# Scratch buffers moved into the weight page, more of V kept between layers, and wo loaded in pieces between two layers

## The chip, the core and the metric

The kernel runs on one core of one Trainium2 chip. The metric is device time in microseconds (us), the median of several executions. The kernel before took 541.6 us (541.54 to 541.95 in five runs). TensorE is called PE here, VectorE DVE, ScalarE ACT, and SyncE, whose queue (SPq) issues the large loads, SP.

## The reference

The reference runs four steps on a single token of width 640, all in bf16: attention, a gated feed-forward block (FFN), and both again with the same weights.

```python
W = min(4096, max(256, Sk // 4))               # 4096 cached positions
k = k_cache[:, :, Sk - W:, :]                  # 32 heads x 4096 x 192
v = v_cache[:, :, Sk - W:, :]
q = (layernorm(x) @ wq), 32 heads of 192
x = x + softmax(q k^T / sqrt(192)) v @ wo
x = x + (silu(layernorm(x) @ w1) * (layernorm(x) @ w3)) @ w2
# ... and the same two lines once more
```

What matters: each layer reads 50.3 MB of K and 50.3 MB of V for one query per head, so nearly all the time goes into reading memory. K and V are the same for both layers. Whatever stays on the core from layer 0 need not be read again in layer 1.

## The kernel before

One large buffer `pg` (the page) holds all loaded data: a ring for weights and seven slots, each for one head pair's K or V (3.15 MB). Loads are queued in a fixed order by `plan`, and all are issued by SP. A load waits until the instructions that use the old contents of its place are done; every load behind it in the queue waits too.

```python
SLOT = 64 * DH
HALF = SLOT // 2
AUX = 10752
RING = AUX + HALF            # the ring runs over the first half of slot 0
NPG = AUX + NSLOT * SLOT
...
def need(key):               # issue the queued loads, in order, up to key
    while key not in place:
        k, at, n, src = queue.pop(0)
        ...
        nc.sync.dma_start(out=pg[:, at:at + n], in_=src)
```

Layer 0 handles head batches 0, 1, 2, 3 and layer 1 handles 3, 2, 1, 0, so the K and V of batch 3 can be kept. The K of batch 3 is kept whole (four slots), V of pairs 1 and 2 whole, V of pair 3 by half, V of pair 0 not at all. The ring overlaps the first half of slot 0, and that is why half of pair 3's V could not stay.

At the start of layer 1 the order of the queue and of PE is this:

```python
for half in (1, 0):                       # wq in ten pieces through the ring
    for c in range(NCH):
        ...plan(("wq", 1, half, c), ring(3072), 3072, ...)
plan_k(1, 2, 0, 1)                        # next K: into slot 1, where K of batch 3 pair 0 lies
plan_v(1, 3, 0, 3)
plan_k(1, 2, 1, 5)
plan_v(1, 3, 3, 0, CUT_V, kept=2)         # the half of V that was not kept
...
plan_cut(("wo", 1, 3), D, (12,), wo_v[3], 0)
...
layernorm()
q_mms(q_ps[1], 1, range(NCH))             # wq second half of the columns
qproj_tail(q_ps[1], 1)
q_mms(q_ps[0], 0, (0, 1))
build_w(order[0])
for z, cs in enumerate(((2, 3), (4,), (), ())):
    k_stage(order[0], z, s_ps, z == 0, z == NZ - 1)   # scores with the kept K, frees its slot
    q_mms(q_ps[0], 0, cs)
```

## Time and profile before

| | before |
|---|---|
| time, median | 541.6 us |
| span of the profiled run | 539.8 us |
| PE, DVE, ACT busy | 54%, 45%, 7% |
| read from HBM | 224.13 MB |
| chain of waits | 69% DMA |

Four lines of the profile's page of the kernel before. The first two belong to the view in 40 slices of 13.5 us: the busy share of the 16 DMA engines in tenths, and what they moved. Then come the bytes read, and the chain of waits by engine.

```profile
DMA  8999999999999999999999899999999999999995
GB/s 352 435 435 433 424 425 431 437 426 430 424 435 421 440 424 429 435 433 424 415 404 414 337 370 420 421 433 433 433 426 427 432 432 430 429 431 426 420 409 206
HBM read 224.13 MB, written 0.00 MB: 415 GB/s over the span
DMA 69%; DVE 13%; PE 12%; ACT 2%; issue 2%; SPq 1%; another core or an unknown queue 0%; ACTq 0%; DVEq 0%
```

The DMA engines are busy nearly all the time. The one place inside the run where they are not is slices 23 and 24 (337 and 370 GB/s, about 297 to 324 us), between the layers. The same stretch in windows of 2 us, of the kernel before; the columns are the window, its length, busy time and instruction counts of PE, PEld, DVE, ACT and POOL, the granted PE clock, the DMA share and GB/s.

```profile
272.00:274.00 2.00, 1.16 (x10) 0.47 (x10) 0.00 (x0) 0.48 (x1) 0.00 (x0) 0.50 0.99 400
274.00:276.00 2.00, 0.97 (x23) 0.83 (x22) 0.90 (x2) 0.00 (x0) 0.00 (x0) 0.50 1.02 420
...
306.00:308.00 2.00, 2.00 (x10) 0.67 (x8) 0.00 (x0) 0.00 (x0) 0.00 (x0) 0.50 0.78 323
308.00:310.00 2.00, 2.00 (x18) 0.80 (x16) 0.00 (x0) 0.00 (x0) 0.00 (x0) 0.85 0.19 73
310.00:312.00 2.00, 2.00 (x20) 0.96 (x16) 0.00 (x0) 0.00 (x0) 0.00 (x0) 1.00 0.51 135
312.00:314.00 2.00, 2.00 (x11) 0.64 (x9) 0.00 (x0) 0.00 (x0) 0.00 (x0) 1.00 0.69 283
314.00:316.00 2.00, 2.00 (x16) 0.76 (x14) 0.00 (x0) 0.00 (x0) 0.00 (x0) 1.00 0.93 393
```

The windows from 300 to 306 us, just before, show 415 to 424 GB/s. Against 420 GB/s the five windows from 306 to 316 us are short by (97 + 347 + 285 + 137 + 27) GB/s x 2 us = 1.79 MB. I call this shortfall "the gap" and work it out from the windows that fall short. A packet is counted whole in the window in which it begins, so a single window is coarse (one below reads 462 GB/s) and the sum over the stretch is what counts. The two windows at 272 us are shown because the change will touch them: here only 0.04 MB is missing there. When SP issued the loads around the gap, from the timeline of the kernel before (start, length, what, how many):

```profile
257.42 25.37 SPq L98 DMA_DIRECT2D pg<-in_B_w_dram  x9
285.30 16.40 SPq L98 DMA_DIRECT2D pg<-in_A_wq_dram  x10
310.46 0.56 SPq L98 DMA_DIRECT2D pg<-in_A_k_cache_dram  x1
```

Between the last wq load (issued by 301.7 us) and the next K load nothing is issued for 8.8 us. The K load needs slot 1, and PE frees it only when the scores of the first kept K block are done.

From 309.5 to 311.8 us no packet begins. The gap is therefore a queue that ran empty, not a slow transfer.

### The profile page before, as it was taken

To read this page: it belongs to the slowest core of one execution; us is meant where nothing else is said; L and a number is where in the kernel's file an instruction comes from. 1 tells how busy PE (TensorE), PEld (TensorE's weight loads), DVE (VectorE), ACT (ScalarE), POOL (GpSimd) and SP (SyncE) were. 2 spreads that over 40 slices of the span, in tenths; PEclk is the share of its full clock that TensorE was granted. 3 is DMA by queue.
4 is the path that set the end of the run, shared out by engine and by line. 5 is a ranking of instruction groups with operands and counts; after the bars stand their busy time and mean duration, and the time that the engine had idled before them with its cause. 6 is when DMAs were issued, how large, how long until landed. Compare 5 with 4: busy or idle time off the path is not lost.

```text
span 539.8 us, 6579 instructions
## 1 busy us (share of the span) xinstructions
PE 292.0 (54%) x2934; PEld 124.8 (23%) x2934; DVE 243.8 (45%) x274; ACT 37.8 (7%) x90; POOL 8.7 (2%) x38
## 2 busy tenths in 40 slices
PE   2427654450774335844456798762763415945365
PEld 1202111110321122213235232220321112312153
DVE  2179974417465265452011026776475075553010
ACT  1000020001100020002010002001100020002000
POOL 6000000000000000000000000000000000000000
PEclk9998797775777757976755599896688757868757
DMA  8999999999999999999999899999999999999995
GB/s 352 435 435 433 424 425 431 437 426 430 424 435 421 440 424 429 435 433 424 415 404 414 337 370 420 421 433 433 433 426 427 432 432 430 429 431 426 420 409 206
DMA packets 15294, 224.56 MB, mean 416 GB/s; under 512 B 1825, under 2 KB 1826, under 8 KB 6690
## 3 DMA queue, kind: packets, MB, share of 16 engines
q1 hardware_dynamic: 15122, 224.14, 97.9%
q8 instruction: 23, 0.38, 0.3%
q14 instruction: 5, 0.04, 0.0%
q10 hardware_dynamic: 144, 0.00, 0.0%
HBM read 224.13 MB, written 0.00 MB: 415 GB/s over the span
## 4 chain that ended last, share of the span: by engine, by line
DMA 69%; DVE 13%; PE 12%; ACT 2%; issue 2%; SPq 1%; another core or an unknown queue 0%; ACTq 0%; DVEq 0%
DMA pg<-in_A_k_cache_dram 51%; DMA pg<-in_A_wo_dram 12%; DVE pg L290 9%; PE s_ps L297 6%; DMA pg<-in_B_w_dram 4%; PE o_ps L340 2%; PE y_ps L372 2%; DMA pg<-in_A_wq_dram 2%; ACT e L315 1%; DVE et L319 1%; SPq L98 1%; DVE wst L282 1%; PE z_ps L437 1%; ACT ptm L328 1%; PE gu_ps L401 0%
## 5 line engine op out<-in xcount | busy, mean ns | idle before, releaser
L290 DVE STREAM_TRANSPOSE pg<-pg 128x1536 uint32<-128x1536 uint32 x112 | 189.2, 1746 | 122.5 <-DMA pg<-in_A_k_cache_dram 122.4
L297 PE MATMUL s_ps<-pg,wst 128*32 128x512 bf16 x768 | 175.5, 618 | 110.1 <-DVE pg L290 107.2
L297 PEld LDWEIGHTS <-wst 128*32 128x32 bf16 x768 | 48.4, 116 | 221.0 <-issue 205.1
L340 PE MATMUL o_ps<-pg,ptm 128*16 128x384 bf16 (+1 forms) x1024 | 73.2, 369 | 23.9 <-DMA pg<-in_A_v_cache_dram 21.0
L340 PEld LDWEIGHTS <-ptm 128*16 128x16 bf16 (+1 forms) x1024 | 30.4, 97 | 53.7 <-issue 39.2
L357 PE MATMUL ot_ps<-o_sb,csel 128*128 128x192 bf16 x16 | 3.5, 317 | 68.2 <-ACT o_sb L354 68.2
L315 ACT ACTIVATE e<-s_ps,nbt 32x512 bf16<-32x512 f32 x16 | 13.1, 821 | 376.6 <-DVE nbt L312 376.4
L372 PE MATMUL y_ps<-otd,pg 128*128 128x1 bf16 x540 | 23.1, 178 | 11.7 <-DVE otd L364 6.8
L372 PEld LDWEIGHTS <-pg 128*128 128x128 bf16 x540 | 23.1, 131 | 13.7 <-issue 9.3
L262 PE MATMUL q_ps<-pg,xs 128*32 128x384 bf16 x160 | 15.9, 491 | 11.6 <-DMA pg<-in_A_wq_dram 8.8
L361 DVE SCALAR_TENSOR_TENSOR om<-ot_ps,rl,dsel 128x192 f32<-128x192 f32 x8 | 3.1, 386 | 36.8 <-PE ot_ps L357 36.8
L349 DVE RECIPROCAL rl<-rl_ps 128x1 f32<-128x1 f32 x8 | 1.4, 169 | 38.7 <-PE rl_ps L347 38.7
L357 PEld LDWEIGHTS <-csel 128*128 128x128 bf16 x16 | 1.6, 100 | 71.8 <-issue 71.8
L319 DVE STREAM_TRANSPOSE et<-e 128x1024 bf16<-128x1024 bf16 x8 | 10.0, 1245 | 15.2 <-ACT e L315 15.2
L328 ACT COPY ptm<-et 32x256 bf16<-32x256 bf16 x32 | 13.6, 425 | 8.0 <-DVE et L319 7.5
L262 PEld LDWEIGHTS <-xs 128*32 128x32 bf16 x160 | 6.2, 123 | 18.7 <-issue 14.1
L303 DVE TENSOR_REDUCE t<-s_ps 128x1 f32<-128x512 f32 x8 | 5.2, 645 | 11.0 <-PE s_ps L297 11.0
L278 DVE CAST qt_sb<-qt_ps 128x96 bf16<-128x96 f32 x4 | 1.0, 257 | 19.6 <-PE qt_ps L275 19.6
L401 PE MATMUL gu_ps<-xs,pg 128*128 128x1 bf16 x120 | 8.1, 200 | 3.0 <-DMA pg<-in_B_w_dram 3.0
L330 DVE COPY ptm<-et 32x256 bf16<-32x256 bf16 x32 | 9.2, 287 | 0.6
L401 PEld LDWEIGHTS <-pg 128*128 128x128 bf16 x120 | 7.7, 166 | 4.1 <-DMA pg<-in_B_w_dram 4.1
L243 PE MATMUL st_ps<-xsq,onesD 128*128 128x12 f32 x8 | 2.4, 374 | 10.7 <-DVE xsq L241 10.7
(66 smaller groups left out, 77.4 us busy)
## 6 DMA issues: line engine op xcount, KB each, us to landing
pg<-in_A_k_cache_dram SPq DMA_DIRECT2D x28, 3072.0 KB, 41.1
pg<-in_A_v_cache_dram SPq DMA_DIRECT2D x27, 3072.0 KB, 37.0
pg<-in_A_wo_dram SPq DMA_DIRECT2D x6, 1920.0 KB, 34.5
pg<-in_A_wq_dram SPq DMA_DIRECT2D x10, 768.0 KB, 8.2
pg<-in_A_wq_dram SPq DMA_DIRECT2D x2, 3072.0 KB, 9.9
pg<-in_B_w_dram SPq DMA_DIRECT2D x8, 768.0 KB, 14.4
pg<-in_A_v_cache_dram SPq DMA_DIRECT2D x3, 1536.0 KB, 16.9
pg<-in_A_wo_dram SPq DMA_DIRECT2D x6, 640.0 KB, 24.1
```

Of the source, the lines that this page charges most:

```text
L98: nc.sync.dma_start(out=pg[:, at:at + n], in_=src)
L262: nc.tensor.matmul(q_ps[32 * j:32 * j + 32, 0:384], lhsT=xs4[:, c, c2, :], rhs=w[:, o:o + 384], start=(c == 0 and cl == 0), stop=(c == NCH ...
L282: nc.vector.tensor_tensor(out=_ap(wst[:], 0, P, 4 + 216 * h, [[433, NZ], [36, 6], [8, 4]]), in0=_ap(qt_sb[:], 0, P, 96 * h + 4 * b, [[1, N ...
L290: nc.vector.transpose(v, v)
L297: nc.tensor.matmul(s_ps[64 * h:64 * h + 32, :], lhsT=wst[:, z, h, it, 4 - 4 * th:36 - 4 * th], rhs=_ap(x, 0, P, 192 * th + 64 * be + par + ...
L315: nc.scalar.activation(out=_ap(e[:], 64 * h, 32, h, [[32, 32], [2, 16]]), in_=s_ps[r, :].rearrange("p (t j) -> p t j", j=16), func=ACTF.Ex ...
L319: nc.vector.transpose(et[:], e[:])
L328: nc.scalar.copy(out=dst, in_=src)
L330: nc.vector.tensor_copy(out=dst, in_=src)
L340: nc.tensor.matmul(o_ps[32 * j:32 * j + mw, 0:384], lhsT=ptm[:, po:po + mw], rhs=x[:, 384 * i:384 * i + 384], start=st, stop=(last and u > ...
L372: nc.tensor.matmul(y_ps[:, c:c + 1], lhsT=w[:, D * i + c:D * i + D:NCH], rhs=od[:, ci:ci + 1], start=(first and ci == 0 and c == 0), stop= ...
L401: nc.tensor.matmul(gu_ps[:, 12 + f:13 + f], lhsT=w[:, FF * cl + f:FF * cl + FF:12], rhs=xs4[:, c, 0, 0:1], start=(c == 0 and f == 0), stop ...
```

## The change

The intent is to read less and to leave the queue less empty. The scratch buffers of the softmax (`ptm`, `e`, `et`) move into the page. They are dead from the end of layer 0's attention until layer 1's first softmax, and in that time the ring uses their place. The ring then no longer overlaps slot 0, so all of V pair 3 stays, and a spare strip keeps four of 64 rows (per partition) of V pair 0. Two of the three pieces of layer 1's first wo go in front of the K load. Piece 1 of wq is used inside the first score block. As the ring overwrites the scratch buffers, a memset zeroes them again in layer 1. The cut below shows the main edits; left out are helpers that plan the places, and a small pool that goes from two buffers to one.

```diff
-HALF = SLOT // 2
-AUX = 10752
+WORK = 4096
+AUX = WORK
+KEPT_T = 4
+KEPT = AUX + 8192 + 3072
+SLOT0 = KEPT + KEPT_T * DH
...
-    plan_ffn(0)
-    for half in (1, 0):
+    plan_ffn(0, ((0, 12288, 3072), (4608, 7680, 10752), (0, 12288, 3072)))
+    for half, ring in ((1, (2, 3, 0, 4, 1)), (0, (2, 3, 0, 4, 1))):
...
+    plan_wo3(1)
+    plan_wo3(2)
     plan_k(1, 2, 0, 1)
-    plan_v(1, 3, 0, 3)
+    plan_v(1, 3, 0, (slot(3), TP - KEPT_T), (None, KEPT_T))
     plan_k(1, 2, 1, 5)
-    plan_v(1, 3, 3, 0, CUT_V, kept=2)
     plan_k(1, 2, 2, 2)
+    plan_wo3(0)
     plan_k(1, 2, 3, 6)
-    plan_cut(("wo", 1, 3), D, (12,), wo_v[3], 0)
...
-    ptm = cst.tile([P, 32 * 64], BF16, name="ptm")
-    e = cst.tile([P, 1024], BF16, name="e")
+    ptm, e, et = pg[:, 0:2048], pg[:, 2048:3072], pg[:, 3072:4096]
...
+    def work_area():
+        live["work"] = (0, WORK)
+        nc.vector.memset(pg[:, 0:3072].bitcast(U32), 0)
...
-            q_mms(q_ps[0], 0, (0, 1))
+            q_mms(q_ps[0], 0, (0,))
             build_w(order[0])
-            for z, cs in enumerate(((2, 3), (4,), (), ())):
-                k_stage(order[0], z, s_ps, z == 0, z == NZ - 1)
-                q_mms(q_ps[0], 0, cs)
+            for z in range(NZ):
+                between = [(3, lambda: q_mms(q_ps[0], 0, (1,)))]
+                k_stage(order[0], z, s_ps, z == 0, z == NZ - 1, between if z == 0 else ())
+                if z == 0:
+                    q_mms(q_ps[0], 0, (2, 3, 4))
+                    work_area()
...
-                steps = "v1 v2 v0 k1 v3 k2 k3"
+                steps = "v1 v2 v3 k1 v0 k2 k3"
```

More of the change, by code (lines that the diff above doesn't have):

```diff
@@ L31 @@
 SLOT = 64 * DH
-HALF = SLOT // 2
-AUX = 10752
+WORK = 4096
[3 more added lines that the diff above has]
+SLOT0 = KEPT + KEPT_T * DH
 NSLOT = 7
-RING = AUX + HALF
-NPG = AUX + NSLOT * SLOT
+NPG = SLOT0 + NSLOT * SLOT
+QCH = 3072
 CUT_Q0 = (2, 2, 1)
@@ L71 @@
     wrk = ctx.enter_context(tc.tile_pool(name="wrk", bufs=1))
-    sml = ctx.enter_context(tc.tile_pool(name="sml", bufs=2))
+    sml = ctx.enter_context(tc.tile_pool(name="sml", bufs=1))
     ps_s = ctx.enter_context(tc.tile_pool(name="ps_s", bufs=1, space=PSUM))
@@ L106, in slot @@
     def slot(s):
-        return AUX + s * SLOT
+        return SLOT0 + s * SLOT
     def kv_src(cache, b, z, t0=0, nt=TP):
@@ L116, with plan_v, cut_v, plan_cut @@
     vkeys = {}
-    def plan_v(layer, b, z, s, cuts=(TP,), kept=0):
+    def plan_v(layer, b, z, *places):
         t = 0
-        keys = vkeys[layer, b, z] = vkeys[0, b, z][len(cuts) - kept:] if kept else []
-        for i, nt in enumerate(cuts[:len(cuts) - kept]):
-            plan(("v", layer, b, z, i), slot(s) + t * DH, nt * DH, kv_src(A_v_cache, b, z, t, nt))
-            keys.insert(i, ("v", layer, b, z, i))
-            t += nt
-    ring_at = [0]
-    def ring(n):
-        if ring_at[0] + n > RING:
-            ring_at[0] = 0
-        ring_at[0] += n
-        return ring_at[0] - n
-    def plan_cut(key, width, cuts, src, at=None):
+        keys = vkeys[layer, b, z] = []
+        for at, nt in places:
+            key = ("v", layer, b, z, t)
+            if at is None:
+                key = ("v", 0, b, z, t)
+            else:
+                plan(key, at, nt * DH, kv_src(A_v_cache, b, z, t, nt))
+            keys.append(key)
+            t += nt
+    def cut_v(s):
+        at, out_ = slot(s), []
+        for nt in CUT_V:
+            out_.append((at, nt))
+            at += nt * DH
+        return out_
+    def plan_cut(key, width, cuts, src, at):
         x = 0
         for i, n in enumerate(cuts):
-            w = n * width
-            plan(key + (i,), ring(w) if at is None else at + x, w, src[:, x:x + w])
-            x += w
-    def plan_ffn(layer, at=(None, None, None)):
+            plan(key + (i,), at[i] if isinstance(at, tuple) else at + x, n * width, src[:, x:x + n * width])
+            x += n * width
+    def plan_ffn(layer, at):
         plan_cut(("w1", layer), FF, CUT_1, w1_v, at[0])
@@ L146 @@
     x = 0
-    for i, (n, at) in enumerate(zip(CUT_Q0, (slot(0), slot(1), 0))):
+    for i, (n, at) in enumerate(zip(CUT_Q0, (slot(0), slot(1), AUX))):
         plan(("wq", 0, i), at, n * H * DH, wq_v[:, x:x + n * H * DH])
@@ L156, with plan_wo3 @@
             plan_k(0, b + 1, z, ks[z])
-            plan_v(0, b, z, vs[z])
-        plan_cut(("wo", 0, b), D, (12,), wo_v[b], 0)
-    plan_v(0, 3, 0, 0)
-    plan_v(0, 3, 1, 6)
-    plan_v(0, 3, 2, 4)
-    plan_v(0, 3, 3, 0, CUT_V)
-    plan_cut(("wo", 0, 3), D, CUT_WO, wo_v[3])
-    plan_ffn(0)
-    for half in (1, 0):
+            plan_v(0, b, z, (slot(vs[z]), TP))
+        plan_cut(("wo", 0, b), D, (12,), wo_v[b], AUX)
+    plan_v(0, 3, 0, (slot(0), TP - KEPT_T), (KEPT, KEPT_T))
+    plan_v(0, 3, 1, (slot(6), TP))
+    plan_v(0, 3, 2, (slot(4), TP))
+    plan_v(0, 3, 3, *cut_v(0))
+    plan_cut(("wo", 0, 3), D, CUT_WO, wo_v[3], AUX)
+    plan_ffn(0, ((0, 12288, 3072), (4608, 7680, 10752), (0, 12288, 3072)))
+    for half, ring in ((1, (2, 3, 0, 4, 1)), (0, (2, 3, 0, 4, 1))):
         for c in range(NCH):
             o = 6144 * c + 3072 * half
-            plan(("wq", 1, half, c), ring(3072), 3072, wq_v[:, o:o + 3072])
+            plan(("wq", 1, half, c), QCH * ring[c], QCH, wq_v[:, o:o + 3072])
+    def plan_wo3(i):
+        w = 4 * D
+        plan(("wo", 1, 3, i), AUX + i * w, w, wo_v[3][:, i * w:i * w + w])
+    plan_wo3(1)
+    plan_wo3(2)
     plan_k(1, 2, 0, 1)
-    plan_v(1, 3, 0, 3)
+    plan_v(1, 3, 0, (slot(3), TP - KEPT_T), (None, KEPT_T))
     plan_k(1, 2, 1, 5)
-    plan_v(1, 3, 3, 0, CUT_V, kept=2)
     plan_k(1, 2, 2, 2)
+    plan_wo3(0)
     plan_k(1, 2, 3, 6)
-    for z in (1, 2):
+    for z in (1, 2, 3):
         vkeys[1, 3, z] = list(vkeys[0, 3, z])
-    plan_cut(("wo", 1, 3), D, (12,), wo_v[3], 0)
     for (b, ks, vs) in ((2, (1, 3, 0, 6), (4, 5, 2, 1)),
@@ L181 @@
             plan_k(1, b - 1, z, ks[z])
-            plan_v(1, b, z, vs[z])
+            plan_v(1, b, z, (slot(vs[z]), TP))
         if b == 2:
-            plan_cut(("wo", 1, b), D, (12,), wo_v[b], 0)
+            plan_cut(("wo", 1, b), D, (12,), wo_v[b], AUX)
     for z, s in enumerate((3, 5, 0)):
-        plan_v(1, 0, z, s)
-    plan_v(1, 0, 3, 2, CUT_V)
-    plan_cut(("wo", 1, 1), D, (12,), wo_v[1], 0)
+        plan_v(1, 0, z, (slot(s), TP))
+    plan_v(1, 0, 3, *cut_v(2))
+    plan_cut(("wo", 1, 1), D, (12,), wo_v[1], AUX)
     plan_cut(("wo", 1, 0), D, CUT_WO, wo_v[0], slot(6))
@@ L290, in k_transpose, with k_scores @@
             nc.vector.transpose(v, v)
-    def k_scores(x, z, s_ps, first, last):
+    def k_scores(x, z, s_ps, first, last, between=()):
+        n = 0
         for th in range(2):
@@ L300, in k_scores @@
                                      tile_position=(0, 64 * h))
+                n += 1
+                for at, emit in between:
+                    if at == n:
+                        emit()
     def softmax_front(s_ps, l):
@@ L314, in softmax_front, with softmax_back @@
             r = slice(64 * h, 64 * h + 32)
-            nc.scalar.activation(out=_ap(e[:], 64 * h, 32, h, [[32, 32], [2, 16]]),
+            nc.scalar.activation(out=_ap(e, 64 * h, 32, h, [[32, 32], [2, 16]]),
                                  in_=s_ps[r, :].rearrange("p (t j) -> p t j", j=16), func=ACTF.Exp,
                                  bias=nbt[r, 0:1], scale=SCALE, accum_out=l[r, :])
-        et = wrk.tile([P, 1024], BF16, tag="w1", name="et")
-        nc.vector.transpose(et[:], e[:])
-        return et
-    def softmax_back(et):
+        nc.vector.transpose(et, e)
+    def softmax_back():
         for h in range(2):
             for a in range(4):
-                dst = _ap(ptm[:], 32 * a, 32, 2 * h, [[64, 32], [20, NZ], [1, 2]])
-                src = _ap(et[:], 64 * h, 32, 8 * a, [[32, 32], [1, NZ], [4, 2]])
+                dst = _ap(ptm, 32 * a, 32, 2 * h, [[64, 32], [20, NZ], [1, 2]])
+                src = _ap(et, 64 * h, 32, 8 * a, [[32, 32], [1, NZ], [4, 2]])
                 if a % 2 == 0:
@@ L359, in combine @@
                              rhs=o_sb[:, 192 * par:192 * par + 192], start=(par == 0), stop=(par == 1))
-        om = wrk.tile([P, 16, 12], F32, tag="w3", name="om")
+        om = wrk.tile([P, 16, 12], F32, tag="w0", name="om")
         nc.vector.scalar_tensor_tensor(out=om[:], in0=ot_ps[:], scalar=rl[:],
@@ L445 @@
     layernorm()
-    for t in (wst, ptm, e):
-        np_ = t[:].shape[0]
-        flat = _ap(t[:], 0, np_, 0, [[1, t[:].free_size()]])
-        nc.vector.memset(flat.bitcast(U32), 0)
+    nc.vector.memset(_ap(wst[:], 0, P, 0, [[1, NZ * 2 * 6 * 36]]).bitcast(U32), 0)
     for t in s_two:
         nc.vector.memset(t[:], 0.0)
+    def work_area():
+        live["work"] = (0, WORK)
+        nc.vector.memset(pg[:, 0:3072].bitcast(U32), 0)
+    work_area()
     for layer in range(2):
@@ L462, in k_ready, with k_stage @@
                 k_transpose(need(kkey(b, z)))
-        def k_stage(b, z, s_ps, first, last):
-            k_scores(need(kkey(b, z)), z, s_ps, first, last)
+        def k_stage(b, z, s_ps, first, last, between=()):
+            k_scores(need(kkey(b, z)), z, s_ps, first, last, between)
             if not (layer == 0 and b == 3):
@@ L501 @@
             qproj_tail(q_ps[1], 1)
-            q_mms(q_ps[0], 0, (0, 1))
+            q_mms(q_ps[0], 0, (0,))
             build_w(order[0])
-            for z, cs in enumerate(((2, 3), (4,), (), ())):
-                k_stage(order[0], z, s_ps, z == 0, z == NZ - 1)
-                q_mms(q_ps[0], 0, cs)
+            for z in range(NZ):
[3 more added lines that the diff above has]
+                    q_mms(q_ps[0], 0, (2, 3, 4))
+                    work_area()
         k_ready(order[1], 0)
         build_w(order[1])
-        et = softmax_front(s_ps, l)
+        softmax_front(s_ps, l)
         s_ps = s_two[1]
@@ L512 @@
             k_stage(order[1], 0, s_ps, True, False)
-        softmax_back(et)
+        softmax_back()
         if layer == 1:
@@ L538 @@
                     rl = row_sums(l)
+            if layer == 0 and nxt is None:
+                del live["work"]
             if nxt is not None:
@@ L543 @@
                 l = ls[:, (bi + 1) % 2:(bi + 1) % 2 + 1]
-                et = softmax_front(s_ps, l)
+                softmax_front(s_ps, l)
                 s_ps = s_two[bi % 2]
@@ L548 @@
             if nxt is not None:
-                softmax_back(et)
+                softmax_back()
             if y_ps is None:
@@ L556 @@
                     times_columns([("wo", layer, 1, 0)], (12,), later, y_ps, False, False)
-                cuts = CUT_WO if b == last_b else (12,)
+                cuts = CUT_WO if b in (last_b, 3) else (12,)
                 times_columns([("wo", layer, b, i) for i in range(len(cuts))], cuts, od, y_ps, bi == 0, bi == NB - 1)
```

## The prediction

> **What bounds it now.** DMA bandwidth. The 40-slice view shows the DMA engines at nine tenths or more in all slices but the first, the last and one between the layers, mostly near 430 GB/s; the DMA part gives 224.1 MB in 539.8 us. The chain of waits is 69% DMA. PE (54%) and DVE (45%) have room. The Trainium skill ("DMA: Bandwidth & Descriptors", Specifications) gives 435 GB/s as the fabric ceiling; this trace agrees (427 to 433 GB/s in the windows of 10 us from 350 to 490 us). Only fewer bytes, or fewer empty stretches, help.
>
> One stretch is empty. In windows of 2 us, DMA falls from 418 GB/s at 304-306 us to 323, 73, 135, 283, 393 and is back at 316 us: short by about 1.9 MB, 4.4 us. The timeline shows why: the last wq loads drain from 307 to 309.3 us, and the next load, K of batch 2, is issued only at 310.46 us, when the score matmuls of the first kept K block have freed its slot. [...]
>
> **What the change does.**
> 1. Bytes. It puts ptm, e and et inside the big page, where the ring of wq, w1, w3, w2 reuses them while they are dead, and so keeps more of layer 0's V of batch 3: the missing half of pair 3 (1.573 MB) and 4 rows of pair 0 (0.197 MB). 1.77 MB at 430 GB/s: -4.1 us, all critical.
> 2. Gap. Two pieces of layer 1's wo for batch 3 (1.31 MB, 3.05 us) move in front of that K load. Their places come free when pieces 0 and 1 of wq's second half are used (about 303 and 306 us), before the queue drains. Scores for pair 0 start about 1 us earlier and carry 0.8 us of wq matmuls, so K is issued near 310.0 us. Of the 4.4 us I expect 1 to 2 left. The four slowest DMA engines (by packet records they drain at 309.3 us) had lost only 2.4 us there, so the gain is 2.3 to 3.4 us; I take 2.9.
> 3. Costs. One more small load and wo in shorter rows: 0.2 us. A memset of 1536 words, about 1.4 us by the 912 ns for 1024 in the trace, on a DVE idle from 304 to 320 us: free. The first w1 load must now wait for the last V matmuls (about 273 us, before 257) with wo queued until about 276.5: just in time, up to 0.7 us at risk. Later the queue is deep (37 to 41 us from issue to landing), so the moved wo piece and V of pair 0 cost nothing.
>
> The tail after the last weight load (about 10 us) doesn't change.
>
> **Prediction:** 541.6 - 4.1 - 2.9 + 0.2 = 534.8 us, range 533.0 to 537.2. Chances: faster by over 2% 0.02, within 2% 0.96, slower 0.02.
>
> **Signs.** HBM read 222.4 MB. Everything up to about 303 us at the same times. In the windows from 306 to 316 us a shortfall under 0.8 MB in place of 1.9. DVE +1.4 us. From 340 us on, the same instructions 6 to 7.5 us earlier and DMA at 430 GB/s to the end.
>
> **What would make it wrong.** A new gap at 273 to 283 us, where the ring now waits for ptm and wo pieces (then nearer 537). V of pair 0 or the second K issued too late behind the shifted wq matmuls (315 to 325 us), so that the gap only moves. Lagging DMA engines that make the gap worth less than its area (535.5). Full recovery gives 533.2.

## More of the kernel before

On one core there is no second die to compare with, so every run quoted here is one that the records class as fast.

The waits of SP from 302 to 312 us, of the kernel before (who waited, for whom, us in total, times, longest), show just this one:

```profile
SPq L98 <- PE s_ps L297: 8.7, 1, 8.7
```

## The result

The changed kernel took 534.0 us (533.6 to 535.75 in seven runs) against 541.6 us. The ratio is 0.9865, with a 95% interval of 0.9855 to 0.9875. Ratios here and below are the mean time of one kernel's fast runs over that of the kernel before's fast runs of the same rounds, so they are not quite the ratio of the medians. To turn a ratio into us I multiply its distance from 1 by 541.7 us: 0.9865 is -7.3 us.

The same four lines of the page, after:

```profile
DMA  8999999999999999999999999999999999999995
GB/s 355 436 426 434 423 433 432 429 430 425 434 427 427 433 429 436 423 429 426 421 393 412 417 402 423 429 426 431 432 428 423 438 431 427 434 426 432 419 408 217
HBM read 222.36 MB, written 0.00 MB: 418 GB/s over the span
DMA 66%; DVE 13%; PE 11%; issue 7%; ACT 2%; SPq 1%; another core or an unknown queue 0%; ACTq 0%; DVEq 0%
```

The low slices 23 and 24 are gone, 1.77 MB less is read, and the rate elsewhere is what it was. (The chain's 7% of "issue" in place of 2% comes mostly from one piece of 24.6 us that ends at 273.1 us and for which the profile shows no releaser; I read nothing from it.) But slice 21 fell from 404 to 393. The windows of the kernel after show both places:

```profile
272.00:274.00 2.00, 1.16 (x10) 0.32 (x9) 0.00 (x0) 0.48 (x1) 0.00 (x0) 0.50 0.81 325
274.00:276.00 2.00, 0.92 (x21) 0.90 (x21) 0.90 (x2) 0.00 (x0) 0.00 (x0) 0.50 0.98 371
...
306.00:308.00 2.00, 2.00 (x14) 0.67 (x11) 0.00 (x0) 0.00 (x0) 0.00 (x0) 0.58 0.99 407
308.00:310.00 2.00, 2.00 (x20) 0.68 (x18) 0.00 (x0) 0.00 (x0) 0.00 (x0) 1.00 1.02 417
310.00:312.00 2.00, 2.00 (x25) 1.08 (x20) 0.93 (x1) 0.00 (x0) 0.00 (x0) 1.00 1.12 387
312.00:314.00 2.00, 2.00 (x12) 0.61 (x10) 0.41 (x1) 0.00 (x0) 0.00 (x0) 1.00 0.81 328
314.00:316.00 2.00, 2.00 (x12) 0.56 (x10) 0.00 (x0) 0.00 (x0) 0.00 (x0) 1.00 1.00 430
```

The gap shrank from 1.79 to (13 + 3 + 33 + 92) x 2 = 0.28 MB, which at 420 GB/s is 3.6 us won. At 272 to 276 us there is a new dip, (95 + 49) x 2 = 0.29 MB against 0.04 MB before, which is 0.6 us lost if it is not made up later. With 4.1 us for the bytes the sum is -7.1 us, near the measured -7.3. That does not prove the terms one by one: the experiments below show that the dip is made up before the gap. SP's issues, and its wait for the scores, after:

```profile
273.13 11.76 SPq L101 DMA_DIRECT2D pg<-in_B_w_dram  x9
286.44 15.70 SPq L101 DMA_DIRECT2D pg<-in_A_wq_dram  x10
303.58 3.21 SPq L101 DMA_DIRECT2D pg<-in_A_wo_dram  x2
310.38 0.55 SPq L101 DMA_DIRECT2D pg<-in_A_k_cache_dram  x1
...
SPq L101 <- PE s_ps L308: 3.9, 1, 3.9
```

The K load is issued at 310.38 us, practically when it was before (310.46). What closed most of the gap is the line above it: two wo loads issued from 303.6 to 306.8 us, while the queue still had wq to move. SP waits for the scores only after that, 3.9 us in place of 8.7. The dip has its line too: the first w1 load (`in_B_w`) now goes out at 273.13 us, after the last V matmuls, where it went out at 257.42 before. By then the queue in front of it was nearly empty (DMA share 0.81).

### The profile page after: what moved, and what is told of

Same layout as the page of the kernel before. It is cut to its first block, busy times and chain, and to the rows that moved or that the text cites. A ratio compares the mean times of both kernels' runs of the same rounds, so it can differ in the third digit from the quotient of the medians.

```text
span 531.9 us, 6590 instructions
## 1 busy us (share of the span) xinstructions
PE 291.4 (55%) x2934; PEld 124.0 (23%) x2934; DVE 244.9 (46%) x274; ACT 37.8 (7%) x90; POOL 8.7 (2%) x38
## 3 DMA queue, kind: packets, MB, share of 16 engines
HBM read 222.36 MB, written 0.00 MB: 418 GB/s over the span
## 4 chain that ended last, share of the span: by engine, by line
DMA 66%; DVE 13%; PE 11%; issue 7%; ACT 2%; SPq 1%; another core or an unknown queue 0%; ACTq 0%; DVEq 0%
DMA pg<-in_A_k_cache_dram 51%; DVE pg L300 9%; DMA pg<-in_A_wo_dram 8%; PE s_ps L308 6%; DMA pg<-in_B_w_dram 5%; DMA pg<-in_A_wq_dram 2%; PE y_ps L385 1%; ACT pg L330 1%; PE o_ps L353 1%; DVE pg L333 1%; DVE wst L292 1%; ACT pg L341 1%; PE z_ps L450 1%; SPq L101 1%; PE gu_ps L414 1%
## 5 line engine op out<-in xcount | busy, mean ns | idle before, releaser
L308 PEld LDWEIGHTS <-wst 128*32 128x32 bf16 x768 | 47.3, 116 | 222.2 <-issue 204.3
L353 PE MATMUL o_ps<-pg 128*16 128x384 bf16 (+1 forms) x1024 | 74.5, 374 | 21.6 <-DMA pg<-in_A_v_cache_dram 18.6
L353 PEld LDWEIGHTS <-pg 128*16 128x16 bf16 (+1 forms) x1024 | 30.9, 97 | 52.2 <-issue 38.8
L330 ACT ACTIVATE pg<-s_ps,nbt 32x512 bf16<-32x512 f32 x16 | 13.1, 821 | 369.2 <-DVE nbt L327 368.9
L333 DVE STREAM_TRANSPOSE pg<-pg 128x1024 bf16<-128x1024 bf16 x8 | 10.0, 1245 | 15.2 <-ACT pg L330 15.2
L341 ACT COPY pg<-pg 32x256 bf16<-32x256 bf16 x32 | 13.6, 425 | 8.0 <-DVE pg L333 7.5
L343 DVE COPY pg<-pg 32x256 bf16<-32x256 bf16 x32 | 9.2, 287 | 0.6
```

What stands on the lines that cost most here:

```text
L308: nc.tensor.matmul(s_ps[64 * h:64 * h + 32, :], lhsT=wst[:, z, h, it, 4 - 4 * th:36 - 4 * th], rhs=_ap(x, 0, P, 192 * th + 64 * be + par + ...
L330: nc.scalar.activation(out=_ap(e, 64 * h, 32, h, [[32, 32], [2, 16]]), in_=s_ps[r, :].rearrange("p (t j) -> p t j", j=16), func=ACTF.Exp, ...
L333: nc.vector.transpose(et, e)
L341: nc.scalar.copy(out=dst, in_=src)
L343: nc.vector.tensor_copy(out=dst, in_=src)
L353: nc.tensor.matmul(o_ps[32 * j:32 * j + mw, 0:384], lhsT=ptm[:, po:po + mw], rhs=x[:, 384 * i:384 * i + 384], start=st, stop=(last and u > ...
```

## The experiments

My theory: the gain is the sum of two separate parts, bytes (about 4.1 us) and gap, and the loads can't run faster. The rivals: the bytes are partly given back because compute takes over as the limit; the gap is worth only what the slowest DMA engines lost in it (2.4 us); the new dip costs nothing because it only shifts idle time to the gap. All kernels gave correct results.

### The changed kernel again

No edit; this is the yardstick.

> The changed kernel again, unedited, as the yardstick on the same chip as the parts. Expected 534.0 us (7.5 us less than before). In its first timing 2 of 8 runs were near 535.7 and the others near 533.9; if that is a property of the kernel, two groups 1.7 us apart should show again, if it was the chip of that job, one group.

Measured: 534.36 us (533.49 to 534.86, four runs), ratio 0.9868 (0.9853 to 0.9883). The two runs near 535.7 of the first timing did not return as a group; the runs spread over 1.4 us. The kernel before spread over only 0.5 us.

### Only the bytes

```diff
-    plan_wo3(1)
-    plan_wo3(2)
     plan_k(1, 2, 0, 1)
...
-    plan_wo3(0)
     plan_k(1, 2, 3, 6)
+    plan_cut(("wo", 1, 3), D, (12,), wo_v[3], AUX)
...
-            q_mms(q_ps[0], 0, (0,))
+            q_mms(q_ps[0], 0, (0, 1))
...      # cut: the wq matmuls stand between the score blocks as before the change, the memset after the second block
```

> Only the bytes: the new layout and the kept V stay, but wo of batch 3 is loaded whole after the K blocks and the wq matmuls stand as before, so nothing fills the gap between the layers. Sum-of-parts theory: -4.1 us for 1.77 MB at 430 GB/s, +0.3 to 0.7 us for the new dip at 272-276 us, so 537.8 to 538.2 us, with the gap of 4.3 us still there (shortfall near 1.8 MB from 306 to 316 us). Rival (the saved bytes are partly given back because compute becomes the limit after the gap): above 539.5 us.

Measured: 537.79 us (536.9 to 538.74), ratio 0.9928 (0.9915 to 0.994), which is -3.9 us. Three windows of this kernel:

```profile
308.00:310.00 2.00, 2.00 (x15) 0.58 (x12) 0.00 (x0) 0.00 (x0) 0.00 (x0) 1.00 0.25 97
310.00:312.00 2.00, 2.00 (x20) 1.05 (x18) 0.56 (x1) 0.00 (x0) 0.00 (x0) 1.00 0.00 0
312.00:314.00 2.00, 2.00 (x12) 0.79 (x10) 0.78 (x1) 0.00 (x0) 0.00 (x0) 1.00 1.18 369
```

The gap is all there (1.69 MB over the five windows), and the bytes are worth what their transfer takes. Compute did not take over: that rival is out.

### Only the gap

```diff
-    plan_v(1, 3, 0, (slot(3), TP - KEPT_T), (None, KEPT_T))
+    plan_v(1, 3, 0, (slot(3), TP))
     plan_k(1, 2, 1, 5)
+    plan_v(1, 3, 3, (slot(0), 32), (None, 16), (None, 16))
...
-    for z in (1, 2, 3):
+    for z in (1, 2):
         vkeys[1, 3, z] = list(vkeys[0, 3, z])
...
-                steps = "v1 v2 v3 k1 v0 k2 k3"
+                steps = "v1 v2 v0 k1 v3 k2 k3"
```

> Only the gap: new layout, two wo pieces in front of the K load, but all the V that the change keeps is loaded again (224.1 MB read as before). Area theory (every engine's idle time in the gap counts): the gap shrank from 1.8 to 0.24 MB, -3.7 us, with the new dip +0.3 to 0.7 us, so 538.2 to 538.6 us. Rival (the lagging DMA engines had lost only 2.4 us in the gap, and they set the end): 539.5 to 540 us.

Measured: 538.33 us (538.0 to 539.49), ratio 0.994 (0.9928 to 0.9953), which is -3.2 us, with 224.13 MB read as before. Two windows:

```profile
310.00:312.00 2.00, 2.00 (x23) 1.31 (x21) 1.17 (x1) 0.00 (x0) 0.00 (x0) 1.00 0.92 338
312.00:314.00 2.00, 2.00 (x11) 0.99 (x9) 0.17 (x1) 0.00 (x0) 0.00 (x0) 1.00 1.02 419
```

The gap is down to 0.19 MB, and the median lies in the range of the area theory. The rival had asked for 539.5 to 540 us. The upper end of this kernel's interval (0.9953, or 539.2 us) does not reach that. So the gap is worth nearer its area than the part that the slowest engines lost. The rival's range counts 0.3 us or more for the dip; without it the rival would say 539.2 us, at the very edge of the interval. The kernels with one and three pieces below decide it more clearly.

Taken as they stand, -3.9 and -3.2 make -7.1 us, and the whole change measured -7.2 to -7.3 us. But both kernels also pay whatever the new layout costs, so the sum counts that twice. The next kernel measures it.

### Neither part: only the new layout

Both edits above together, on the changed kernel.

> Neither part: only the new layout (ptm, e and et in the page, the new ring, the memset in layer 1), all V loaded again, wo whole and late. It has the dip at 272-276 us (idle near 0.4 us per DMA engine) and the old gap. If the dip costs what it shows: 541.9 to 542.3 us. If it is taken back later: 541.6 us. If the memset or the places in the page cost more than that: above 542.6 us.

Measured: 542.21 us (541.85 to 542.86), ratio 1.0011 (0.9998 to 1.0023), which is +0.6 us, with zero just inside the interval. Windows of this kernel:

```profile
272.00:274.00 2.00, 1.11 (x10) 0.46 (x10) 0.00 (x0) 0.48 (x1) 0.00 (x0) 0.50 0.83 331
274.00:276.00 2.00, 0.92 (x21) 0.73 (x19) 0.90 (x2) 0.00 (x0) 0.00 (x0) 0.50 0.97 333
...
312.00:314.00 2.00, 2.00 (x16) 0.74 (x12) 1.34 (x1) 0.00 (x0) 0.00 (x0) 1.00 0.67 197
```

The dip is short by 0.35 MB here. In this profile (its slowest run) the gap also ended later, with K issued at 311.79 us, and it is 2.07 MB in place of 1.79. The memset shows as DVE's single 1.34 us instruction at 312 us; DVE has nothing else to do there, so the trace shows nothing that it holds up. The layout alone thus costs 0.6 us, with anything from nothing to 1.2 us inside the interval. That this is the dip's cost is not shown: by the packet records of the load queue (packets counted by the share that lies before a given time) this run was 0.34 MB behind the kernel before at 276 us, 0.23 MB at 304 us and 0.56 MB at 316 us, so that most of its loss came in the later gap.

With this kernel the parts can be taken in both orders. The bytes are worth 4.5 us without the gap filled (0.9928 against 1.0011) and 4.0 us with it (0.9866, the mean of the changed kernel's three calls, against 0.994). The gap is worth 3.8 us (0.994 against 1.0011) and 3.4 us (0.9866 against 0.9928). Each of these four carries about 1 us either way, from the intervals of the ratios. With the layout counted once, the parts make -3.9 - 3.2 - 0.6 = -7.7 us, 0.4 us more than was measured, which is within that scatter.

### The first w1 load not waiting for the scratch buffers

```diff
-    plan_ffn(0, ((0, 12288, 3072), (4608, 7680, 10752), (0, 12288, 3072)))
-    for half, ring in ((1, (2, 3, 0, 4, 1)), (0, (2, 3, 0, 4, 1))):
+    plan_ffn(0, ((12288, 0, 3072), (4608, 7680, 10752), (12288, 0, 3072)))
+    for half, ring in ((1, (2, 3, 4, 0, 1)), (0, (2, 3, 4, 0, 1))):
```

> The changed kernel with the places of the first two w1 (and w2) pieces exchanged: the first w1 load goes where nothing was, so that it need not wait for the last V matmuls, and only the second does. The dip at 272-276 us (short by about 0.28 MB, 0.65 us) should be gone. If the dip costs what its area says: 533.3 to 533.5 us, 0.5 to 0.7 under the changed kernel of this call. Rival (the dip only moves idle time that would else come at 310-314 us, as the K load there waits for PE): within 0.2 us of it.

Measured: 534.28 us (533.94 to 534.62), ratio 0.9863 (0.985 to 0.9877): not to be told from the changed kernel's 0.9868.

```profile
272.00:274.00 2.00, 1.30 (x10) 0.37 (x10) 0.00 (x0) 0.48 (x1) 0.00 (x0) 0.50 1.01 412
274.00:276.00 2.00, 0.95 (x25) 1.01 (x26) 0.90 (x2) 0.00 (x0) 0.00 (x0) 0.50 1.02 416
```

The edit did what it should: the dip is gone. Yet by the packet records this kernel was 0.26 MB ahead of the changed one at 276 us, 0.04 MB at 290 us and 0.01 MB at 304 us. From 276 to 290 us the DMA engines were as busy in both (share 1.01 and 1.02), but moved 395 GB/s here and 410 in the changed kernel; why is not shown. SP issued the third wq load at nearly the same time in both (290.04 and 290.16 us). So the lead was used up before the gap: with a remnant of the gap left, removing the dip won nothing that can be measured.

The same count shows something that the dip does not explain. At 304 us the kernel before had moved 128.50 MB. All thirteen profiles of kernels with the new layout had moved less, 128.22 to 128.39 MB, and those without the dip are among them (128.27, 128.34 and 128.36 MB). That is 0.3 to 0.7 us at 420 GB/s, against a single profile of the kernel before. If the layout costs its 0.6 us, the loss is as likely there as in the dip; what causes it was not tested. The last experiments return to the dip with the gap closed.

### One wo piece in front of K, not two

```diff
     plan_wo3(1)
-    plan_wo3(2)
     plan_k(1, 2, 0, 1)
...
     plan_wo3(0)
+    plan_wo3(2)
     plan_k(1, 2, 3, 6)
```

> The changed kernel with only one of the two wo pieces in front of the K load (the other goes later with the third). Fill theory: each piece is worth its 1.5 us of transfer as long as the queue is empty without it, so the gap keeps about 1.9 to 2.1 us of idle time and the time is 1.5 to 1.7 us above the changed kernel: 535.5 to 535.9 us. Rival (the first piece does nearly all, as it bridges the lag between DMA engines): within 0.6 us of the changed kernel.

Measured: 535.53 us (535.33 to 535.99), ratio 0.9889 (0.9873 to 0.9904), which is 1.2 us more than by the changed kernel's mean ratio (from other calls).

```profile
308.00:310.00 2.00, 2.00 (x20) 0.68 (x18) 0.00 (x0) 0.00 (x0) 0.00 (x0) 1.00 0.78 312
310.00:312.00 2.00, 2.00 (x24) 1.14 (x21) 1.10 (x1) 0.00 (x0) 0.00 (x0) 1.00 0.82 221
312.00:314.00 2.00, 2.00 (x12) 0.49 (x8) 0.24 (x1) 0.00 (x0) 0.00 (x0) 1.00 0.68 283
```

The gap is 0.90 MB: 0.62 MB more than with two pieces, and one piece is 0.655 MB. The median lies in the range of the fill theory. The difference of 1.2 us is below its 1.5 to 1.7, but the rival's 0.6 us is further off. Together with the kernel with only the bytes (no piece in front) and the one with three pieces (further below) this makes a series. The gap goes 1.69, 0.90, 0.28 and about 0.06 MB, and the ratio 0.9928, 0.9889, 0.9866 and 0.9849: the pieces win 2.1, 1.2 and 0.9 us, where the shrinking gap gives 1.9, 1.5 and 0.5 us at 420 GB/s. From none to three that is 4.3 us, with intervals of about 0.9 us either way, against the 2.4 us that the slowest engines had lost. The new layout and the kept V are in all four, so this does not depend on what they cost. (The kernel with no piece in front also lacks the interleaved wq piece; leaving that out alone, as the next experiment does, costs 0.4 us.)

### Without the interleaved wq piece

```diff
-            q_mms(q_ps[0], 0, (0,))
+            q_mms(q_ps[0], 0, (0, 1))
...
-                between = [(3, lambda: q_mms(q_ps[0], 0, (1,)))]
-                k_stage(order[0], z, s_ps, z == 0, z == NZ - 1, between if z == 0 else ())
+                k_stage(order[0], z, s_ps, z == 0, z == NZ - 1)
```

> The changed kernel without the interleaving: wq piece 1 is used before the scores of pair 0 start, as in the kernel before. My prediction said the scores start about 1 us earlier thanks to it and K is issued 0.45 us earlier. In the changed kernel's trace K was issued only 0.08 us earlier. Expected: K issued within 0.5 us of the changed kernel, time within 0.4 us of it, because wo piece 2 is released earlier and the queue stays full.

Measured: 534.75 us (534.36 to 535.53), ratio 0.9873 (0.986 to 0.9886), 0.4 us over the changed kernel's mean ratio, and the intervals overlap. K was issued at 310.93 us, against 310.38, 310.70 and 311.07 us in three profiles of the changed kernel. The interleaving does little that these runs can resolve.

### All three wo pieces in front of K

```diff
-    for half, ring in ((1, (2, 3, 0, 4, 1)), (0, (2, 3, 0, 4, 1))):
+    for half, ring in ((1, (2, 3, 0, 4, 1)), (0, (2, 3, 4, 0, 1))):
...
-        plan(("wo", 1, 3, i), AUX + i * w, w, wo_v[3][:, i * w:i * w + w])
+        plan(("wo", 1, 3, i), AUX + i * w if i else 4 * QCH, w, wo_v[3][:, i * w:i * w + w])
...
     plan_wo3(2)
+    plan_wo3(0)
     plan_k(1, 2, 0, 1)
...
-    plan_wo3(0)
     plan_k(1, 2, 3, 6)
...
-                between = [(3, lambda: q_mms(q_ps[0], 0, (1,)))]
+                between = [(3, lambda: q_mms(q_ps[0], 0, (1,))), (8, lambda: q_mms(q_ps[0], 0, (2,)))]
...
-                    q_mms(q_ps[0], 0, (2, 3, 4))
+                    q_mms(q_ps[0], 0, (3, 4))
```

> The changed kernel with all three wo pieces in front of the K load; the third takes the place of wq piece 2, which is used in the middle of the scores. It adds 1.5 us of transfer, and K is issued about 0.6 to 0.8 us later. If idle DMA time in the gap (0.46 us per engine in the changed kernel) is what is left to win: idle near 0, and 0.3 to 0.5 us faster than the changed kernel, 533.5 us. If the later K or V load opens a new gap behind it: slower by 0.3 us or more.

Measured: 533.0 us (532.65 to 534.79), ratio 0.9846 (0.9831 to 0.986).

```profile
308.00:310.00 2.00, 2.00 (x18) 0.84 (x16) 0.00 (x0) 0.00 (x0) 0.00 (x0) 1.00 1.00 413
310.00:312.00 2.00, 2.00 (x22) 1.14 (x20) 0.72 (x1) 0.00 (x0) 0.00 (x0) 1.00 1.03 415
312.00:314.00 2.00, 2.00 (x12) 0.47 (x9) 0.61 (x1) 0.00 (x0) 0.00 (x0) 1.00 1.20 462
```

The gap is closed, and the gain is larger than the 0.3 to 0.5 us that were expected; K was issued at 310.58 us, 0.2 us later than in the first profile of the changed kernel (0.6 to 0.8 were expected) and no later than in its other profiles. As the changed kernel had run in another call, I ran both again on one chip.

### The same two on one chip

> The changed kernel again, on the chip of the next two, as their yardstick: 533.5 to 534.9 us as before.

Measured: 534.39 us (534.12 to 534.78), ratio 0.9866 (0.9851 to 0.988). The profile taken here is of the 534.78 us run:

```profile
310.00:312.00 2.00, 2.00 (x29) 1.33 (x27) 0.23 (x1) 0.00 (x0) 0.00 (x0) 1.00 0.70 278
312.00:314.00 2.00, 2.00 (x12) 0.56 (x8) 1.10 (x1) 0.00 (x0) 0.00 (x0) 1.00 0.91 302
```

In this run K was issued at 311.07 us, 0.7 us later than in the 533.61 us run, and the gap was 0.53 MB in place of 0.28. This is where at least part of the changed kernel's spread comes from: a remnant of the gap that varies from run to run (0.25 MB, or 0.6 us, of the 1.2 us between these two runs).

> The version with all three wo pieces in front of the K load, again, beside the changed kernel. If its lead is real: 0.5 to 1.2 us faster than the changed kernel of this call, about 533 us. If the lead was a difference between the chips: within 0.3 us.

Measured: 533.22 us (532.48 to 534.58), ratio 0.9852 (0.9836 to 0.9868), 0.8 us less than the changed kernel. Before, this version was 1.1 us below the changed kernel's mean ratio. The intervals of one call overlap, but both calls point the same way.

### Three pieces and the exchanged places together

Both edits, with the rings `((1, (2, 3, 4, 0, 1)), (0, (2, 3, 4, 0, 1)))`.

> Three wo pieces and the exchanged w1 and w2 places together. With the gap closed, no idle time at 310 us is left to hide what the dip at 272 us cost. If the dip costs its 0.4 us now: 0.3 to 0.5 us faster than the version with three pieces alone. If the DMA engines take it back before 304 us, as in the earlier exchange: within 0.25 us of it.

Measured: 532.73 us (532.35 to 533.18), ratio 0.9835 (0.982 to 0.9849).

> The version with three wo pieces and the exchanged places, once more on another chip or job. If its lead is real, the ratio to the kernel before is again 0.983 to 0.985 (the changed kernel had 0.9865 to 0.9868 in three calls); if it was scatter, 0.985 to 0.986, as the three pieces alone.

Measured: 532.92 us (532.4 to 533.29), ratio 0.9837 (0.9824 to 0.9851).

This is the best version, 8.9 us under the kernel before and 1.6 us under the changed one. Its lead over the version with three pieces alone is 0.7 us by the mean ratios (0.9836 against 0.9849). That would fit "the dip costs its time once no gap is left", but the traces do not show it: by 304 us this version had moved 128.27 and 128.34 MB in its two profiles, the three-piece version 128.22 and 128.28 MB, and the profiled runs were no faster (533.18 and 532.51 us against 532.80 and 532.48). The difference is that the three-piece version had two runs in eight near 534.7 us and this one none in nine. Without these two the means are 532.93 and 532.80 us. Whether the exchange prevents such runs, or none fell among nine by chance, is not settled.

## Why the prediction was right, point by point

The predicted time was 534.8 us, in a range of 533.0 to 537.2, and 534.0 us was measured. "Within 2%" held.

- **The bound.** Right. But for the exchanges of places, the experiments follow the bytes moved and the stretches in which the DMA engines stood idle. None shows PE or DVE as the limit after the gap. PE matters in one place: it sets when the K load may start.
- **Bytes, -4.1 us.** Right: 222.36 MB were read (222.4 predicted), and the term measured 4.0 and 4.5 us in the two orders (about 1 us either way).
- **Gap, -2.9 us.** The mechanism was right, the size probably too small: 3.4 and 3.8 us, each within about 1 us, and 3.6 us by the area in the traces. The step that failed is "The four slowest DMA engines ... had lost only 2.4 us there, so the gain is 2.3 to 3.4 us". Nearly the whole area of the gap counted: filling it with three pieces won 4.3 us. I also expected 1 to 2 us of it to be left; 0.28 MB, or 0.7 us, was.
- **K issued near 310.0 us.** Wrong: 310.38, 310.70 and 311.07 us in three profiles, 310.46 before. The scores did start 1.0 us earlier (303.89 us against 304.86), but with the wq matmuls among them it took 0.9 us longer until K was issued. The prediction's own numbers, 1 us earlier with 0.8 us of matmuls added, give 0.2 us and not 0.46. Undoing the interleaving moved the time by 0.4 us, within the intervals. The fill did the work, not the earlier scores.
- **Costs, +0.2 us, and the dip "just in time, up to 0.7 us at risk".** The dip came: 0.29 MB. What it cost is not shown, as it was made up by 304 us. The layout alone measured +0.6 us (interval -0.1 to +1.2), for which the sum has nothing. If that is real, this error and that of the gap term have opposite signs and nearly cancel, and it is partly luck that the total came so close. The +0.2 us was not tested.
- **"Everything up to about 303 us at the same times."** Wrong from 272 us on: first the dip, then 0.15 MB less moved by 304 us, and the last wq load issued at 301.81 us in place of 301.38.
- **Memset free.** Consistent with the trace: 1338 ns at 311 us, on a DVE with nothing else to do until 321 us. DVE's busy time rose by 1.1 us (1.4 predicted). It was not tested by itself; the layout-only kernel bounds it together with the dip.
- **After 340 us the same loads 6 to 7.5 us earlier.** Nearly: the first wo load of the last group was issued at 466.79 us, where it was 474.33 us before, 7.5 us earlier, and the output 7.9 us earlier (529.74 against 537.61 us). The profiled run was one of the fastest.

## What to carry to other kernels

In a kernel whose loads fill the whole run, look for the few windows in which the queue is empty, find which place in memory the next load waits for, and put loads in front of it whose places are already free; each is worth about its transfer time until the gap is full (here 2.1, 1.2 and 0.9 us for pieces of 1.6 us each at 420 GB/s, the last with only 0.28 MB left to fill). Memory shared between scratch buffers and loads buys bytes, but the first load into such a place inherits a wait for the last reader. Giving that place to a load that is not first in line removed the dip here; that this saves time was not shown. A total that comes out right can hide two wrong terms, and only kernels with one part each show it.

## What the Trainium skill lacked or had wrong

- "Perfetto Trace Analysis", section "What "DMA-bound" means", names DMA engines, the issuing sequencer and SBUF reads as limits. This section does not list the case met here: all engines idle inside a DMA-bound run because the next load's place is not yet free. (The page's general advice, to look for what blocks the busiest engine, does lead to it.) In the kernel before that was 1.79 MB, or about 4 us of 541.6.
- "DMA: Bandwidth & Descriptors", section "Latency and other measured facts", gives about 0.6 us to the first byte for loads issued by SP. In the kernel before, the K load's issuing instruction began at 310.46 us and lasted 0.56 us, and the first packet began at 311.81 us. That is 0.8 us from the end of the issue and 1.35 us from its start, from which one plans a load. Both are longer than the page's figure, and the section does not say from where it counts.
- The same page, section "Specifications", gives 435 GB/s as the fabric ceiling; the runs agree (427 to 433 GB/s in windows of 10 us from 350 to 490 us in the kernel before). With weight loads (wq packets of 6,144 bytes, where K has 24,576), from 280 to 300 us, the DMA engines were just as busy and moved 401 to 413 GB/s. The cause of that was not tested.
- "VectorE: DVE Perf Modes", section "Zero memsets can be issued as uint32 (trn2)", says one cycle per element. With the 0.96 GHz of "Trainium Kernel Development and Optimization" (section "NeuronCore Architecture") that is an estimated 1.60 us for 1536 words. The trace has 1.338 us: 16% shorter than the pages say. The traces also have 0.912 us for 1024 words, 0.778 for 864, 0.485 for 512 and 0.325 for 320. All five lie on 59 ns plus 0.833 ns per word, where one cycle at 0.96 GHz would be 1.04 ns.
